# Third entry's first step two steps later, one piece a step; filter copy in 4 transfers

## The chip, the cores and the metric

The kernel runs on one core of one Trainium2 chip. The metric is the device time of a whole execution in microseconds (us). The kernel before has a median of 1882.88 us over 4 runs (1879.95, 1881.62, 1884.13 and 1885.79).

A core has engines with their own instruction queues: TensorE (PE, matmuls, with its weight loads PEld), VectorE (DVE), ScalarE (ACT), GpSimd (POOL) and SyncE (SP). Each works through its queue strictly in order; semaphores join the queues. SP, ACT and POOL also issue DMA transfers. Matmuls write to PSUM, from where ACT or DVE must copy results out before the buffer can be used again.

## The reference

Two computations follow each other. The first mixes along the sequence: a real Fourier transform, a product with a complex filter, and the inverse. The second is a feed-forward block with a SoLU activation and a layer norm.

```
X = rfft(x, axis=1)                       # x: 8 entries x 3136 x 256, f32
y = irfft(X * (filt_r + 1j * filt_i))     # filter: 1569 x 256, the same for all entries
h = y.reshape(25088, 256) @ w_in          # 25088 x 1024
solu = h * softmax(h)
ln = (solu - mean) / sqrt(var + 1e-6) * g_ln
out = ln @ w_out                          # 25088 x 256
```

## The kernel before

**The transform.** The length 3136 is split as 49 x 64 and the transform of an entry is done as matmuls in three stages with DRAM between them. *First* (L171): a load of x gives a piece of 98 rows x 4 columns x 256 channels; two matmul tiles (halves u = 0 and 1, PSUM tile `pa`) multiply it with a table, ACT copies each to SBUF (L180), and POOL stores the piece to the DRAM tile d1 (L183). An entry has 8 pieces. *Spectrum* (L189 to L241), 25 units of an entry's columns: a load of d1 (L193, SP), a forward matmul (`pb`), the product with the filter (ACT turns the parts at L214 and L215, DVE multiplies and adds at L222 to L224), an inverse matmul (`pc`), a copy by ACT (L236) and a store to the DRAM tile d2 (L241, POOL). A unit of two entries, or two units of one entry, go together. *Back* (L253): 8 pieces of d2 are loaded by SP, multiplied (`py`, two tiles a piece) and copied by ACT (L261) into the SBUF tile y, which holds two entries.

**The feed-forward part** goes over 196 blocks of 128 tokens, one a *step* k of the loop at L550. `hidden(k)` is 4 matmuls into h (L415), the maximum on DVE (L420) and the exponential on ACT (L423). `normalize(k)` is the product on DVE (L438) and the squares on ACT (L440). `turn` and `regroup` transpose over DVE and 4 small SP transfers (L448, L457), 4 to 5 steps later; `project(k - 6)` is 8 matmuls of the output (L475), so steps 0 to 5 have no projection. `prepare_w_out` scales the output weights on DVE in step 0, takes their mean on PE in step 1 (L383), and subtracts it on DVE in step 2.

**What comes when.** Entries 0 and 1 (group 0) run through first and spectrum before the loop, and entry 0 through back too, inside the block at L267, which also loads the weights as float64 words and converts them to float32 on DVE (`load_float64`, L280 to L300, ten instructions for a quarter of a weight matrix). The output weights are the four conversions j = 4 to 7; their loads (L275) are issued by POOL. In this block a scheduler of the framework orders the instructions of each engine; it sees the whole program, and it may take instructions from behind the block forward when nothing holds them. The loop stands under `tc.manual_schedule()`: there the order is as written.

In the loop the other entries' stages are spread over the steps. `GROUPS` (L37) gives for groups 1 to 4 the entries, (start, steps) of their first stage and (start, steps) of their spectrum; `spread(count, start, over)` puts piece i at step start + i * over // count. The jobs of a step come in this order: `first_of` (only steps 0 to 5: both halves of a piece and both halves of a back piece), hidden, turn, regroup, `early` (half 0), project, normalize, scale, then products, `late` (half 1), `stores` and `loads`. A load of rows is issued three steps ahead, or when the fourth load before it has been used: x pieces and back pieces share one pool of 4 buffers. PSUM has two tiles (`ps_t`) for `pa`, `py` and `pc` together, and SBUF two buffers for a first-stage result.

The filter is also needed in the loop, in an order of its own: L503 to L509 copy it from the inputs to the DRAM tile `f_dram`, in groups of 5 of the 25 planes, real and imaginary, upper and lower half, so 20 DRAM-to-DRAM transfers of 160 KB, four in each of steps 0 to 4, issued by POOL. `load_filter` (L399) reads it two steps before a unit's product.

Of the kernel before, what the change touches and what calls it, by code (L numbers as in the profile page):

```python
# [17 lines left out]
P = 128  # L18
B, S, C = 8, 3136, 256
# [5 lines left out]
NS, NQ = (N1 + 1) // 2, 64  # L25
NR = 2 * N1
NK = 4 * NS
NG = 5
# [7 lines left out]

GROUPS = [  # L37
    ((0, 1), None, None),
    ((2,), (0, 6), (9, 13)),
    ((3, 4), (6, 13), (22, 25)),  # L40
    ((5, 6), (32, 28), (64, 29)),
    ((7,), (94, 18), (116, 24)),
]
# [37 lines left out]
def kernel(  # L81
# [10 lines left out]
    nc = tc.nc  # L92
# [19 lines left out]
    f_dram = dram.tile([NS, NQ, 2, C], FP32, name="f_dram")  # L112
# [23 lines left out]
    def filter_rows(filt, quarter, s0, n):  # L136

        off, step = (s0 * C, C) if quarter % 2 == 0 else ((N1 - s0) * C, -C)
        return bass.AP(tensor=filt.tensor, offset=filt.offset + off,
                       ap=[[N1 * C, 32], [step, n], [1, C]])  # L140
# [104 lines left out]
    def fetch_back(e, ch, rows_pool):  # L245

        n, b = next((n, g[0].index(e)) for n, g in enumerate(GROUPS) if e in g[0])
        t4s[e, ch] = rows_pool.tile([P, NCH, C], FP32, name=f"t4_{e}_{ch}", tag="r")[0:NK]
        by_16(
            (nc.sync.dma_start, nc.sync.dma_start), t4s[e, ch],  # L250
            d2[n][b].rearrange("s (a n) c -> (s a) n c", a=4)[:, NCH * ch:NCH * ch + NCH, :])

    def back(e, ch, cb, evac):  # L253

        ps = ps_t.tile([P, 512], FP32, name=f"py_{e}_{ch}_{cb}", tag="t")
        psv = ps[:, 0:NCH * NR].rearrange("p (n r) -> p n r", r=NR)
        for i in range(NCH):
            nc.tensor.matmul(out=psv[:, i, :], lhsT=t4s[e, ch][:, i, cb * P:cb * P + P],  # L258
                             rhs=wi_t, start=True, stop=True)
        n0, t0 = NCH * ch, e % 2 * S  # L260
        evac(out=y[:, cb, t0:t0 + S].rearrange("p (r n) -> p n r", n=NH)[:, n0:n0 + NCH, :], in_=psv)  # L261
# [217 lines left out]
    def scale(k, ps):  # L479
# [14 lines left out]
    first_of, early, products, late, stores, loads = (  # L494
        [[] for _ in range(blocks + LAG)] for _ in range(6))

    def spread(count, start, over):
        return [start + i * over // count for i in range(count)]
# [1 line left out]
    def ahead(t, by):  # L500
        return loads[max(0, t - by)]

    for g in range(NS // NG):  # L503
        for k, filt in enumerate((filt_r, filt_i)):
            for half in range(2):
                loads[g].append(lambda filt=filt, half=half, k=k, g=g: nc.gpsimd.dma_start(
                    out=f_dram[NG * g:NG * g + NG, 32 * half:32 * half + 32, k, :].rearrange(
                        "s p c -> p s c"),
                    in_=filter_rows(filt, half, NG * g, NG)))  # L509

    row_loads = []

    for n in range(1, len(GROUPS)):
# [16 lines left out]
            stores[t + 1].append(lambda sp=sp, i=i: sp.store(i, nc.gpsimd.dma_start))  # L530
    for e in range(1, B):

        start, end = -(-S * (e - 1) // P) + (3 if e == 3 else 1), S * e // P - 1
        for ch, t in enumerate(spread(NH // NCH, start, end - start)):
            row_loads.append((t, lambda e=e, ch=ch: fetch_back(e, ch, pools["r"])))
            for cb in range(KD):
                (first_of if t < LAG else (early, late)[cb])[t].append(
                    lambda e=e, ch=ch, cb=cb: back(e, ch, cb, nc.scalar.copy))
# [62 lines left out]
```

## Time and profile before

| | us |
|---|---|
| median of 4 runs | 1882.88 |
| the profiled execution, its time | 1879.95 |
| its span, first to last instruction | 1878.0 |
| PE busy | 1801.0 (96%) |
| DVE busy | 1111.9 (59%) |
| ACT busy | 816.6 (43%) |
| POOL busy | 456.5 (24%) |
| start of the products of the first spectrum | 78.57 |
| start of the back matmuls of entry 0 | 147.93 |
| start of the first hidden matmul (step 0) | 181.25 |

The profiled execution is the lowest of the four runs. A step is recognised by its 8 records of L415 (a 128x512 f32 matmul makes two records of 429 ns start to start). In the table of windows, a row gives a stretch, its length, and the busy time of each engine with its number of records, then the clock that TensorE was granted (1.00 is full), the share of the DMA engines' time in use, and GB/s. A row of the timeline gives start, length, engine, line, operation, the tile written and those read, shapes, how many records are merged, and in brackets how long the engine had been idle and who released it. A row of waits gives the waiting engine and line, whom it waited for, the sum in us, how often, and the longest.

### The profile page before, as it was taken

What the parts mean: (1) busy time and instruction counts of PE and PEld (TensorE: products, weight loads), DVE (VectorE), ACT (ScalarE), POOL (GpSimd) and SP (SyncE); (2) the same over time, 40 slices, a digit from 0 to 9 for tenths busy, and PEclk for the clock granted to TensorE, in tenths of its full rate; (3) what the DMA queues carried; (4) which work ended last, traced back from release to release, by engine and by line L of the source; (5) the groups of instructions that cost most, each with busy time, mean ns of one, the idle gap of its engine ahead of it and who ended that gap; (6) DMA issues with size and microseconds to landing.
All of it is one profiled execution on the core that took longest, in us unless ns stands there. A gap on an engine that the chain in (4) does not pass through costs nothing.

```text
span 1878.0 us, 21235 instructions
## 1 busy us (share of the span) xinstructions
PE 1801.0 (96%) x6500; PEld 1166.4 (62%) x6500; DVE 1111.9 (59%) x1778; ACT 816.6 (43%) x1329; POOL 456.5 (24%) x1306
## 2 busy tenths in 40 slices
PE   6678899999999999999999999999999999999997
PEld 1126466666666666666666666666777676666665
DVE  0792445567666654566666655566665655666663
ACT  2363445544554534354554434444444343333331
POOL 3331333323323221132232121213222011110110
PEclk9796899999999999999999999999999999999999
DMA  9875489886778766566657656466684444434434
GB/s 276 276 228 159 141 227 253 235 196 165 197 198 206 186 148 149 133 160 167 165 147 177 147 132 156 100 162 158 159 181 112 112 93 111 114 83 101 103 89 101
DMA packets 314576, 300.77 MB, mean 160 GB/s; under 512 B 27602, under 2 KB 278995, under 8 KB 314465
## 3 DMA queue, kind: packets, MB, share of 16 engines
q1 hardware_dynamic: 283904, 206.69, 47.0%
q0 software_dynamic: 28768, 86.45, 15.5%
q10 hardware_dynamic: 1792, 6.29, 0.9%
q8 instruction: 53, 0.87, 0.2%
q14 instruction: 59, 0.48, 0.1%
HBM read 118.44 MB, written 81.40 MB: 106 GB/s over the span
## 4 chain that ended last, share of the span: by engine, by line
PE 90%; DMA 4%; issue 2%; POOL 1%; DVE 1%; ACT 1%; SPq 0%; POOLq 0%; DVEq 0%; ACTq 0%
PE po L475 36%; PE h L415 35%; PE py L258 7%; PE pa L177 5%; PE pb L203 4%; PE pc L233 3%; DMA x<-in_x_dram 2%; POOL d L241 1%; DMA d<-t 1%; DMA t<-d 1%; DVE nmax L420 0%; ACT e L423 0%; DVE solu L438 0%; ACT t L180 0%; POOL f L310 0%
## 5 line engine op out<-in xcount | busy, mean ns | idle before, releaser
L475 PE MATMUL po<-w_out_sb,solu_t 128*128 128x256 f32 x3136 | 713.4, 381 | 4.5 <-DVE ot L483 4.5
L415 PE MATMUL h<-w_in_sb,y 128*128 128x512 f32 x1568 | 707.7, 594 | 0.0
L475 PEld LDWEIGHTS po<-w_out_sb,solu_t 128*128 128x128 f32 x3136 | 593.7, 191 | 137.4 <-issue 57.4
L420 DVE TENSOR_REDUCE nmax<-h 128x1 f32<-128x1024 f32 x196 | 239.8, 1223 | 450.7 <-PE h L415 450.7
L415 PEld LDWEIGHTS h<-w_in_sb,y 128*128 128x128 f32 x1568 | 294.5, 191 | 314.6 <-issue 304.2
L423 ACT ACTIVATE e<-h,nmax 128x1024 f32<-128x1024 f32 x196 | 218.4, 1114 | 603.3 <-DVE nmax L420 603.3
L440 ACT ACTIVATE e<-solu,nmu 128x1024 f32<-128x1024 f32 x196 | 225.1, 1148 | 293.9 <-DVE solu L438 287.8
L438 DVE SCALAR_TENSOR_TENSOR solu<-e,rsum,h 128x1024 f32<-128x1024 f32 x196 | 251.0, 1281 | 7.1 <-DVE rsum L435 0.2
L448 DVE STREAM_TRANSPOSE turn<-solu 128x1024 f32<-128x1024 f32 x196 | 241.9, 1234 | 0.0
L241 POOL DMA_DIRECT2D d<-g x101 | 76.0, 753 | 565.8 <-ACT g L236 555.4
L258 PEld LDWEIGHTS py<-wi_t,t 100*128 100x128 f32 x1024 | 146.7, 213 | 59.6 <-issue 41.7
L177 PE MATMUL pa<-x,wf_t 98*100 98x512 f32 x256 | 140.8, 657 | 27.1 <-DMA x<-in_x_dram 20.5
L258 PE MATMUL py<-wi_t,t 100*128 100x98 f32 x1024 | 146.3, 295 | 16.5 <-DMA t<-d 9.2
L467 POOL COPY rs_t<-rs 32x1 f32<-32x1 f32 x784 | 141.7, 181 | 35.7
L483 DVE TENSOR_SCALAR ot<-po,rs_t 128x256 f32<-128x256 f32 x196 | 94.5, 482 | 84.0 <-PE po L475 73.0
L222 DVE TENSOR_TENSOR p<-pb,f 128x512 f32<-128x512 f32 (+1 forms) x101 | 69.2, 686 | 122.3 <-ACT i L215 121.1
L203 PE MATMUL pb<-t,de 128*128 128x512 f32 (+1 forms) x250 | 107.2, 527 | 13.7 <-DMA t<-d 13.0
L261 ACT COPY y<-py 128x392 f32<-128x392 f32 x128 | 106.8, 835 | 30.4 <-PE py L258 30.3
L461 POOL TENSOR_SCALAR rs<-var 128x4 f32<-128x4 f32 x49 | 9.6, 197 | 451.7 <-ACT e L440 449.9
L233 PE MATMUL pc<-p,de 128*128 128x512 f32 (+1 forms) x250 | 103.8, 513 | 9.7 <-DVE p L224 8.2
L177 PEld LDWEIGHTS pa<-x,wf_t 98*100 98x100 f32 x256 | 44.9, 183 | 89.9 <-issue 59.5
L180 ACT COPY t<-pa 100x512 f32<-100x512 f32 (+1 forms) x112 | 71.1, 640 | 65.6 <-PE pa L177 59.3
(51 smaller groups left out, 853.1 us busy)
## 6 DMA issues: line engine op xcount, KB each, us to landing
solu_t<-turn SPq DMA_DIRECT2D x784, 128.0 KB
t<-d SPq DMA_DIRECT2D x99, 256.0 KB
d<-g POOLq DMA_DIRECT2D x99, 256.0 KB, 4.1
out_dram<-ot SPq DMA_DIRECT2D x196, 128.0 KB
x<-in_x_dram SPq DMA_DIRECT2D x64, 384.0 KB
t<-d SPq DMA_DIRECT2D x64, 384.0 KB
d<-t POOLq DMA_DIRECT2D x48, 384.0 KB, 5.1
f<-f_dram POOLq DMA_DIRECT2D x104, 128.0 KB, 4.3
```

The lines of the kernel that those rows point to most:

```text
L177: nc.tensor.matmul(out=ps[0:NK, j], lhsT=wf_t, rhs=self.xs[i][0:NR, 2 * u:2 * u + 2, :], start=True, stop=True)
L203: nc.tensor.matmul(out=ps[:, w * j:w * j + w, :], lhsT=de[:, s + j, 0, :], rhs=t2[:, w * j:w * j + w, :], start=True, stop=True)
L233: nc.tensor.matmul(out=ps[:, w * j:w * j + w, :], lhsT=de[:, s + j, 1, :], rhs=pt[:, w * j:w * j + w, :], start=True, stop=True)
L258: nc.tensor.matmul(out=psv[:, i, :], lhsT=t4s[e, ch][:, i, cb * P:cb * P + P], rhs=wi_t, start=True, stop=True)
L415: nc.tensor.matmul(out=h[:, half, :], lhsT=y[:, c, P * t:P * t + P], rhs=w_in_sb[:, c, 512 * half:512 * half + 512], start=(c == 0), stop= ...
L420: nc.vector.tensor_reduce(out=nmax, in_=h, axis=AX.X, op=ALU.max, negate=True)
L423: nc.scalar.activation(out=e, in_=h, func=AFT.Exp, bias=nmax, accum_out=esum)
L438: nc.vector.scalar_tensor_tensor(out=solu, in0=e, scalar=rsum, in1=hs.pop(k), op0=ALU.mult, op1=ALU.mult, accum_out=nmu)
L440: nc.scalar.activation(out=e, in_=solu, func=AFT.Square, bias=nmu, scale=-float(DFF), accum_out=variances[g][:, i:i + 1])
L448: nc.vector.transpose(out=turns[g][:, :, i, :], in_=solus.pop(k).rearrange("p (f j) -> p f j", j=32))
L467: nc.gpsimd.tensor_copy(out=rss[g][32 * i:32 * i + 32, c:c + 1], in_=rs[32 * c:32 * c + 32, i:i + 1])
L475: nc.tensor.matmul(out=ps, lhsT=solu_t[:, f, :], rhs=w_out_sb[:, f, :], start=(f == 0), stop=(f == KF - 1))
```

## The change

Three things are altered in the loop's plan:

- Entry 2 (group 1): its first stage moves from (0, 6) to (2, 7). The pieces stood at steps 0, 0, 1, 2, 3, 3, 4, 5; they now stand at 2, 2, 3, 4, 5, 6, 7, 8. Its spectrum moves from steps 9 to 21 to steps 11 to 23.
- Entries 3 and 4 (group 2): first from (6, 13) to (9, 13), spectrum from steps 22 to 46 to steps 24 to 48. The back pieces of entry 2 begin at step 27 instead of 26, those of entry 3 at 53 instead of 52.
- `f_dram` is written by 4 transfers of 800 KB, one in each of steps 0 to 3, instead of 20 of 160 KB.

```
 GROUPS = [
     ((0, 1), None, None),
-    ((2,), (0, 6), (9, 13)),
-    ((3, 4), (6, 13), (22, 25)),
+    ((2,), (2, 7), (11, 13)),
+    ((3, 4), (9, 13), (24, 25)),
     ((5, 6), (32, 28), (64, 29)),
...
-    for g in range(NS // NG):
-        for k, filt in enumerate((filt_r, filt_i)):
-            for half in range(2):
-                loads[g].append(lambda filt=filt, half=half, k=k, g=g: nc.gpsimd.dma_start(
-                    out=f_dram[NG * g:NG * g + NG, 32 * half:32 * half + 32, k, :].rearrange(
-                        "s p c -> p s c"),
-                    in_=filter_rows(filt, half, NG * g, NG)))
-
+    def copy_filter(k, half):
+        nc.gpsimd.dma_start(
+            out=f_dram[:, 32 * half:32 * half + 32, k, :].rearrange("s p c -> p s c"),
+            in_=filter_rows((filt_r, filt_i)[k], half, 0, NS))
+
+    for k in range(2):
+        for half in range(2):
+            loads[2 * k + half].append(lambda k=k, half=half: copy_filter(k, half))
...
-        start, end = -(-S * (e - 1) // P) + (3 if e == 3 else 1), S * e // P - 1
+        start, end = -(-S * (e - 1) // P) + {2: 2, 3: 4}.get(e, 1), S * e // P - 1
```

The built program shows one more difference, ahead of the loop. The scheduler's order for the first spectrum is another one: on POOL, the two copies of the filter's real part are taken forward, one before the first store of L241 and one between the 15th and the 16th; on POOL, the loads of the last two quarters of the output weights come earlier (behind the 12th and the 18th store instead of behind the 15th and the last); on DVE, 17 more of the conversion instructions stand before the last product of the first spectrum (33 instead of 16, with 9 behind it instead of 26); on ACT, copies of L236 stand in bunches of three where they alternated with L214 and L215. In step 0 the first x piece is no longer loaded ahead of the back pieces of entry 0.

## The prediction

> **What bounds the kernel now.** I read the page's first two parts, then the windows cut at the starts of the steps, then PE's timeline where a window is not full, and last the waits of DVE, PE and ACT in the first spectrum. From the page:
>
> ```profile
> span 1878.0 us, 21235 instructions
> PE   6678899999999999999999999999999999999997
> ```
>
> and from the windows (all engines; then PE alone, for steps 0, 1, 2, 4, 6 and 7):
>
> ```profile
> 78.57:137.49 58.92, 48.62 (x95) 15.80 (x94) 56.83 (x94) 42.06 (x72) 23.70 (x34) 0.98 0.74 229
> 252.43:1838.70 1586.27, 1585.76 (x5914) 1053.48 (x5913) 976.47 (x1542) 706.77 (x1161) 376.63 (x1153) 1.00 0.63 153
> ...
> 181.25:194.66 13.41, 8.85 (x29) 0.85 0.67 211
> 194.66:204.65 9.99, 9.99 (x29) 0.86 0.36 107
> 204.65:219.68 15.03, 10.62 (x34) 0.89 0.56 159
> 224.86:231.23 6.37, 5.40 (x14) 1.00 0.08 33
> 234.66:252.43 17.77, 15.55 (x49) 0.81 0.87 212
> 252.43:261.07 8.64, 8.64 (x30) 1.00 0.98 299
> ```
>
> From step 7 to the last hidden matmul PE is busy 1585.76 of 1586.27 us at full clock. Step 7 lasts 8.64 us and holds 8 records of 429 ns (hidden), 16 of 216 (projection) and 4 of 429 (pa), 8.60 in all: matmuls back to back. The change alters no matmul, so in this stretch it can only add waits. What it can win or lose lies before 252.43: in the first spectrum, where DVE is busy 56.83 of 58.92 us and so sets the pace, and in steps 0 to 6, where PE is not full. The timeline there:
>
> ```profile
> 136.81 0.67 DVE L224 TENSOR_TENSOR p<-p,i 128x512 f32<-128x512 f32 x1
> 137.41 0.68 DVE L292 SCALAR_TENSOR_TENSOR power<-raw,power 128x512 int32<-128x512 int32 x1
> 151.25 0.69 DVE L300 TENSOR_TENSOR w_out_sb<-w_out_sb,power 128x512 f32<-128x512 f32 x1
> ...
> 147.93 27.60 PE L258 MATMUL py<-wi_t,t 100*128 100x98 f32 x128 [9.20 <-DMA t<-d]
> 175.32 6.09 PE L177 MATMUL pa<-x,wf_t 98*100 98x512 f32 x8
> 191.13 3.74 PE L258 MATMUL py<-wi_t,t 100*128 100x98 f32 x16 [4.56 <-ACT t L180]
> 194.66 4.99 PE L415 MATMUL h<-w_in_sb,y 128*128 128x512 f32 x8
> 214.38 3.66 PE L177 MATMUL pa<-x,wf_t 98*100 98x512 f32 x4 [4.41 <-ACT t L180]
> 242.19 2.03 PE L258 MATMUL py<-wi_t,t 100*128 100x98 f32 x8 [2.21 <-ACT t L180]
> 244.01 5.91 PE L475 MATMUL po<-w_out_sb,solu_t 128*128 128x256 f32 x16
> ```
>
> The last product of the first spectrum is at 136.81; DVE then still converts weights until 151.94, which nobody waits for, while the last product goes through pc, a copy, a store (issued at 139.64, landed 2.7 us later) and the load to py at 147.93. In the steps the brackets show one pattern: two tiles fill `ps_t`, ACT frees them only behind that step's exponential and squares, and PE stands 4.56, 4.41, 0.97 (step 4) or 2.21 us. After the long ones PE runs at half clock: py x16 takes 3.74 instead of 1.99, h 4.99 instead of 3.60, pa 3.66 instead of 1.88, py x8 2.03 instead of 1, po 5.91 instead of 3.62. Waits in the first spectrum (78 to 140 us):
>
> ```profile
> DVE p L222 <- ACT i L215: 6.8, 9, 5.0
> PE pc L233 <- DVE p L224: 7.2, 15, 1.2
> ACT g L236 <- DMA d<-g: 1.0, 1, 1.0
> ```
>
> DVE's own idle time inside the stretch is 1.8 us (6.8 less the 5.0 before its first product): it has no room for more work.
>
> **A. The first spectrum.** As built, the changed program puts 17 more conversion instructions before the last product: 6 of the second conversion (692, 421, 418, 687, 686 and 685 ns by the groups of 139 to 152 us), all 10 of the third (5.30 us) and one of the fourth (421 ns), 9.3 us by their lengths. DVE starts the next 0.60 us after a long one and 0.34 after a short one where they are mixed with others: 8 x 0.60 + 9 x 0.34 = 7.9. I take 8.0; at most 9.3, at least 6.1 if all of the 1.8 us is filled. The cover is gone by the same move: behind 137 us these instructions ran beside the store and the load. Everything to the first hidden matmul (back of entry 0, 27.60 us of PE) moves by as much.
>
> Three smaller terms. (1) ACT now does three copies of L236 in a row with three buffers, so the next waits for a store's landing, which took 2.5 to 6.4 us (median 3.9) in this stretch; DVE waits behind. Also an 800 KB copy now runs beside the loads and stores, at a DMA share of 0.74 that was 0.94 to 1.00 from 90 to 100 us. One such wait cost 1.0 before; I take +1.8, between 0 and 4. (2) Where 7 to 9 conversions stand between products, PE gets gaps of 2.5 to 3 us instead of at most 1.4. Gaps of 2.21 and more cost the clock in the steps; a pc at half clock takes 2.06 instead of 1.10. I take two spells, +2.2; 0 to 5. (3) The last weight load no longer stands before the last loads, whose landing decided 147.93: -1.0; 0 to -1.5. Sum A: 8.0 + 1.8 + 2.2 - 1.0 = +11.0, ends 4.6 and 18.3.
>
> [...]
>
> **B. Steps 0 to 9.** Lost before: idle 4.56 + 4.41 + 0.97 + 2.21 = 12.2, half clock 1.75 + 1.39 + 1.78 + 1.03 + 2.29 = 8.2, together 20.4. The 8 pa records before step 0 (6.09 us for 3.43 of work) paid the end of the half clock; the first hidden matmuls take their place and pay it alike.
>
> Lost after, from the same durations, counted from the end of the first hidden (its end to the weights' scaling is nmax 1.23, exp 1.30, rsum 0.6, product 1.38, scaling 2.1, some 6.5):
> - Step 1: py 1.8 and hidden 3.43 end at 5.2; the mean over the weights waits to 6.5: 1.3 idle.
> - Step 2 has two pieces, four tiles: the third waits for ACT behind squares 1 and the weights' mean: 1.7.
> - Step 3 has pa, pa, py, py: the pattern of step 0 before, 4.6 idle and 3.1 at half clock.
> - Step 5: as step 4 before, 1.0.
> - Step 9 has two pa and a py, as step 6 before: 2.2, without the half clock, since a projection follows on either side.
>
> Sum 13.9. So B = 13.9 - 20.4 = -6.5. At best (no half clock, step 9 at 0.9) 9.3 is lost, B = -11.1; at worst a second and longer half-clock spell, 19.8, B = -0.6. Moving three pieces from the loose steps to steps 6 to 8 costs their 5.2 us there and frees it here, already in this count.
>
> **C. The filter copy itself.** 20 issues of 0.58 to 0.65 us were 11.8 us of POOL, beside waits of POOL on ACT of up to 38.5 us; 4 issues cost between 2.4 and 12 us. PE never waited for them: 0. Their first reader moves from step 7 to 9. [...] In this trace they land in 3.6 to 6.3 us, several at a time, and nobody waits.
>
> **D. The later stages.** The first load of a spectrum now stands in the step of its last piece's store (steps 8 and 21), as does the first back load of entry 2 (step 24, the store of the last unit). On SP it waits for copy, two POOL issues and landing, 0.6 + 1.1 + 4 to 7 us into the next step; behind it are that step's 4 regroup transfers (2.6 to 5.6 us of issue), whose projection comes two steps later, after 8.6 + 8.6 + 3.5 us. 21 against 9 to 14 and their landing: I take 0, at worst 5.
>
> **Sum.** 11.0 - 6.5 + 0 + 0 = +4.5. Against the profiled execution (1879.95, its span and 1.95 around it) 1884.4. That execution is 2.9 below the median; the half-clock spells that make up 8 us of its loss need not fall alike in every run, so I carry the difference to the median: 1882.88 + 4.5 = 1887.4. Within 0.2% is 3.8 us either way, about what a measurement here can tell from no change.
>
> **Rivals.** *The two cancel.* The order on DVE costs its 8 less 1, the clock holds in the spectrum and ACT's bunches cost nothing: A = 7, B = -6.5 to -8: 1882 to 1883. For it: PE kept full clock from 82 to 144 us before, through gaps of up to 1.4 us. Against it: the gaps double.
> *The steps win (other side).* One mechanism: PE's stands behind ACT vanish and with them the half clock, B = -11, while A is no more than its bare 7: -4, 1879; it decides from A below B's size less 3.8. For it: 8.2 us of half clock hang on three stands, of which one remains. Against it: one pattern of 4.6 is kept.
> *SP stands.* If a landing takes 7 us and regroup's issue 5.6 at steps 21 to 25, a projection comes late, up to three times: +5 to +10 on top, 1892 to 1897. For it: issues of 5.2 to 5.6 us at 270 to 330 us. Against it: 21 us of room.
> *The change does not do what it says:* the copies in 4 leave POOL free, but it was free; that is C, zero in every case.
>
> **Numbers.** Forecast (slower by 2 to 9 us) 0.44, SP 0.06, cancel 0.28, steps win 0.22. Slower 0.50, same 0.28, faster 0.22. The range leaves a tenth on either side: from 1878, between the steps-win case and the ends of B, to 1895, A's upper part with B at -3.
>
> **What would show it.** A: the first py of entry 0 starts at about 159 instead of 147.93, the last L224 at about 147, and DVE's conversions end near 152 as before. B: the first hidden matmul follows py at once; step 0 to 6 have one stand over 4 us (step 3, <-ACT t L180), short ones of 1 to 2; step 6 near 9 us. D: no PE wait for solu_t after step 9, step lengths equal to their matmuls. I am wrong if py starts before 153 (DVE had room), if half clock shows in 80 to 140 us for more than 10 us (A larger), or if windows after step 9 are not full.

## The result, and the profile after

The changed kernel has a median of 1889.86 us over 47 runs (1883.24 to 1897.80), the kernel before 1884.58 over 74 runs beside them (1879.21 to 1890.71). The ratio is 1.0026 with a 95% interval of 1.0020 to 1.0032: slower by 4.9 us (3.8 to 6.0), where +4.5 was forecast, 1887.4 against 1882.88. The profiled execution has a span of 1888.7 us, 10.7 more than that of before; what part of the 10.7 belongs to the change is the first thing to settle.

The first spectrum, as windows (length, busy time of PE, PEld, DVE, ACT, POOL with records, then granted clock, DMA share, GB/s). The first row runs from the first `pb` to the end of the last product, the second from there to the first `py` of entry 0; then steps 0 to 3 by their places in the profile (a place begins at the step's first hidden matmul and ends at the next one's, so the next step's `first_of` is its tail), then steps 9 and 13, and the rest:

```profile
span 1888.7 us, 21209 instructions
...
79.75:155.22 75.47, 57.24 (x98) 19.48 (x98) 65.28 (x111) 42.94 (x74) 25.91 (x37) 0.87 0.65 209
155.22:165.43 10.21, 1.10 (x3) 0.33 (x3) 4.63 (x10) 0.58 (x1) 0.72 (x1) 0.63 0.72 211
192.82:199.34 6.52, 6.52 (x25) 3.73 (x25) 1.23 (x1) 1.11 (x2) 0.00 (x0) 0.80 0.01 3
199.34:212.36 13.02, 10.59 (x34) 5.84 (x33) 7.62 (x19) 7.82 (x14) 1.06 (x2) 1.00 0.23 62
212.36:225.62 13.26, 8.85 (x30) 5.53 (x28) 6.67 (x14) 4.82 (x8) 3.69 (x7) 0.76 0.70 215
225.62:232.76 7.14, 7.14 (x14) 2.97 (x14) 1.52 (x2) 1.03 (x2) 0.00 (x0) 0.72 0.55 173
270.19:283.99 13.80, 12.43 (x49) 7.49 (x48) 4.47 (x7) 6.26 (x12) 1.86 (x4) 1.00 0.64 152
314.29:327.70 13.41, 12.32 (x43) 7.37 (x42) 6.28 (x11) 6.48 (x11) 3.08 (x6) 1.00 1.05 269
327.70:1849.00 1521.30, 1520.79 (x5672) 1010.51 (x5671) 939.67 (x1484) 676.32 (x1111) 358.02 (x1099) 1.00 0.62 151
```

The same first window of before:

```profile
75.28:137.48 62.20, 51.91 (x98) 16.76 (x98) 56.82 (x94) 43.23 (x74) 23.69 (x34) 0.95 0.74 230
```

DVE has 111 records instead of 94, the 17 conversion instructions, and is busy 8.46 us longer; the stretch is 13.27 longer, so DVE is idle 4.81 us more (10.19 instead of 5.38). PE's clock is 0.87 instead of 0.95, and its 98 matmuls take 57.24 instead of 51.91. The waits of DVE and of PE in it (sum, times, longest):

```profile
DVE p L222 <- ACT i L215: 10.5, 6, 8.7
DVE p L222 <- PE pc L233: 4.8, 7, 1.0
...
PE pc L233 <- ACT g L236: 10.9, 5, 2.9
```

The middle row is new, 4.8 us, as much as the added idle time: DVE stands because `pc`, which reads the buffers of the products, is not through. `pc` in turn waits for ACT's copies out of PSUM, 10.9 us where it was 1.4 before. PE's timeline shows where, and what it costs behind (start, length, line, tiles, records merged, idle before):

```profile
102.77 3.32 PE L233 MATMUL pc<-p,de 128*128 128x512 f32 x4 [2.66 <-ACT g L236]
...
115.20 1.98 PE L233 MATMUL pc<-p,de 128*128 128x512 f32 x4 [2.90 <-ACT g L236]
...
127.64 3.42 PE L233 MATMUL pc<-p,de 128*128 128x512 f32 x4 [2.31 <-ACT g L236]
...
145.32 3.78 PE L233 MATMUL pc<-p,de 128*128 128x512 f32 x4 [2.76 <-ACT g L236]
...
165.43 27.60 PE L258 MATMUL py<-wi_t,t 100*128 100x98 f32 x128 [8.96 <-DMA t<-d]
192.82 4.92 PE L415 MATMUL h<-w_in_sb,y 128*128 128x512 f32 x8
...
210.57 1.96 PE L177 MATMUL pa<-x,wf_t 98*100 98x512 f32 x4 [2.43 <-ACT t L180]
...
222.09 3.73 PE L258 MATMUL py<-wi_t,t 100*128 100x98 f32 x16 [4.41 <-ACT t L180]
...
326.76 1.10 PE L177 MATMUL pa<-x,wf_t 98*100 98x512 f32 x2 [1.09 <-ACT g L236]
```

Four records of `pc` take about 1.9 us at full clock (1.90 at 90.56). Behind three of these four stands (a stand is a time in which PE waits) they take 3.32, 3.42 and 3.78 at a granted clock of 0.57, 0.57 and 0.50; behind the longest one, at 115.20, they take 1.98 at 1.00. DVE's waits for `pc` go with the clock and not with the length of the stand:

```profile
104.42 0.69 DVE L222 TENSOR_TENSOR p<-pb,f 128x512 f32<-128x512 f32 x1 [0.43 <-PE pc L233]
...
129.75 0.69 DVE L222 TENSOR_TENSOR p<-pb,f 128x512 f32<-128x512 f32 x1 [0.61 <-PE pc L233]
131.10 0.69 DVE L222 TENSOR_TENSOR p<-pb,f 128x512 f32<-128x512 f32 x1 [0.66 <-PE pc L233]
...
147.43 0.69 DVE L222 TENSOR_TENSOR p<-pb,f 128x512 f32<-128x512 f32 x1 [0.52 <-PE pc L233]
149.13 0.69 DVE L222 TENSOR_TENSOR p<-pb,f 128x512 f32<-128x512 f32 x1 [1.01 <-PE pc L233]
```

These five, 3.2 us, stand behind the three slow ones. The other two (1.04 at 88.38 and 0.47 at 91.69) are at the start of the stretch, where a `pc` of two records at 86.20 still took 2.08 us at a clock of 0.50. Behind the `pc` at 115.20 DVE has no wait for it.

From 192.82 on, PE's rows show the steps: hidden directly behind `py`, one stand of 2.43 at the two pieces of step 2, one of 4.41 with half clock (0.50) behind it in step 3, and one of 1.09 in step 13.

By stage, after against before:

| stage | before | after | difference |
|---|---|---|---|
| up to the first `pb` | 75.28 | 79.75 | +4.5 |
| first `pb` to first `py` of entry 0 | 72.65 | 85.68 | +13.0 |
| first `py` to the start of step 10 | 132.99 | 118.56 | -14.4, of which -6.0 is work moved behind step 10 (12 pa and 4 pb records: 12 x 0.429 + 0.86) |
| step 10 to the end | 1597.10 | 1604.68 | +7.6, of which +6.0 is that work |

So the first spectrum gives +13.0, steps 0 to 9 give -8.4, and something behind step 10 gives +1.6: +6.2. The remaining +4.5 lies in front of the first `pb`, where the instruction order of both programs is the same; the second profile of the changed kernel, below, has it at -1.7. The +6.2 is a difference of two single profiles, and the medians differ by less (4.9 by the ratio): the profiled execution of before is one of its faster ones.

### The profile page after: what moved, and what is told of

The parts are those of the page before. It is cut to its first block, busy times and chain, and to the rows that moved or that the text cites. A ratio compares the mean times of both kernels' runs of the same rounds, so it can differ in the third digit from the quotient of the medians.

```text
span 1888.7 us, 21209 instructions
## 1 busy us (share of the span) xinstructions
PE 1806.3 (96%) x6500; PEld 1167.8 (62%) x6500; DVE 1111.6 (59%) x1778; ACT 815.5 (43%) x1329; POOL 446.8 (24%) x1290
## 4 chain that ended last, share of the span: by engine, by line
PE 89%; DMA 4%; issue 2%; DVE 2%; POOL 1%; ACT 1%; SPq 0%; DVEq 0%; ACTq 0%; POOLq 0%
PE po L475 35%; PE h L415 35%; PE py L258 7%; PE pa L177 5%; PE pc L233 4%; PE pb L203 4%; DMA d<-t 2%; DMA x<-in_x_dram 1%; POOL d L241 1%; DMA t<-d 1%; DVE nmax L420 1%; DMA d<-g 0%; DVE solu L438 0%; ACT e L423 0%; ACT t L180 0%
## 5 line engine op out<-in xcount | busy, mean ns | idle before, releaser
L475 PEld LDWEIGHTS po<-w_out_sb,solu_t 128*128 128x128 f32 x3136 | 592.0, 190 | 136.8 <-issue 57.5
L241 POOL DMA_DIRECT2D d<-g x101 | 75.4, 747 | 576.8 <-ACT g L236 564.4
L233 PE MATMUL pc<-p,de 128*128 128x512 f32 (+1 forms) x250 | 108.4, 537 | 15.1 <-ACT g L236 10.9
```

The lines of the kernel that those rows point to most:

```text
L233: nc.tensor.matmul(out=ps[:, w * j:w * j + w, :], lhsT=de[:, s + j, 1, :], rhs=pt[:, w * j:w * j + w, :], start=True, stop=True)
L475: nc.tensor.matmul(out=ps, lhsT=solu_t[:, f, :], rhs=w_out_sb[:, f, :], start=(f == 0), stop=(f == KF - 1))
```

## Experiments

All ratios are against the kernel before, run beside them. "Between" is the number of conversion instructions that DVE has between the first and the last product (before 16, changed 33). Two explanations of the first spectrum's loss are set against each other: the *order theory* (where the conversions stand on DVE costs it) and the *traffic theory* (the copies' bytes beside the spectrum's loads and stores cost it). The first four runs undo or separate the parts of the change, the rest vary the order or the number of copies, and two take a second profile of a program. Times from "first `pb` to last product" end at the start of the last product; the windows end with it.

**The copy alone.** The old `GROUPS` and starts, with `copy_filter` in steps 0 to 3. The scheduler leaves the first spectrum as it was.

```
-    ((2,), (2, 7), (11, 13)),
-    ((3, 4), (9, 13), (24, 25)),
+    ((2,), (0, 6), (9, 13)),
+    ((3, 4), (6, 13), (22, 25)),
...
-{2: 2, 3: 4}.get(e, 1)
+(3 if e == 3 else 1)
```

> Only the filter's DRAM copy is changed (4 transfers of 800 KB in steps 0 to 3); entry 2's pieces stay where they were, and the order of the first spectrum is that of before (26 conversion instructions behind the last product, no copy taken forward). The order theory and the traffic theory both put the loss into the first spectrum and the gain into the steps, so both expect no change: 0, within 2 us, and the first py of entry 0 some 72 to 73 us after the first pb. The rival that four long copies cost time by themselves in the loop (POOL's queue, DMA bandwidth in steps 0 to 9) expects the whole difference of the change here, +4.9 us.

Measured: 1.0007 (0.9997 to 1.0018), no difference that can be told. First `pb` to first `py` took 73.3 us, and the stands of before are all there (4.57, 4.41, 0.97 and 2.22).

**The moved stages alone.** The new `GROUPS` and starts, with the 20 transfers of before.

> Only the stages are moved; the copy stays in 20 transfers of 160 KB. The scheduler takes 8 of them (1.28 MB, against 1.6 MB in the changed kernel) forward into the first spectrum, but puts only one more conversion instruction before the last product instead of 17. Order theory (DVE's place for the conversions costs the +13.0 us of the first spectrum): 13.0 / 17 = +0.8 there, -8.4 in the steps, so -7.6 us against before, about 1877; first py 73 to 74 us after the first pb. Traffic theory (the copies beside the spectrum's loads and stores cost it): 13.0 x 1.28 / 1.6 = +10.4, in all +2.0, about 1886.5; first py about 83 us after the first pb.

Measured: 0.9963 (0.9949 to 0.9976), -7.0 us. The window from the first `pb` to the end of the last product:

```profile
75.97:138.19 62.22, 52.25 (x98) 16.76 (x98) 57.49 (x95) 43.05 (x74) 28.61 (x42) 0.95 0.78 245
```

One record more on DVE, eight more on POOL (the 1.28 MB of copies that were taken forward), the DMA share up from 0.74 to 0.78, and the length is that of before. The copies' bytes cost nothing that can be seen here; the traffic theory falls for this place. With the first run this makes the table of two by two: copy alone +0.07%, stages alone -0.37%, both +0.26%. The loss belongs to neither part. It comes out of the order that the scheduler finds when both are there.

**The copies two steps later.** The changed kernel with one line altered:

```
-            loads[2 * k + half].append(...)
+            loads[2 + 2 * k + half].append(...)
```

> As the changed kernel, but the four copies stand in steps 2 to 5 instead of 0 to 3. None is taken forward, and the conversions stand as before (26 behind the last product). Both theories say that the loss of the first spectrum is gone and the gain of steps 0 to 9 stays: -8.4 us against before, about 1876 (ratio 0.9955), first py 72 to 73 us after the first pb, first hidden matmul directly behind py, lost time in steps 0 to 9 about 15 us against 23.6. The rival that the moved steps themselves cost the first spectrum its time (the x loads that no longer stand ahead of the back pieces) expects no gain: +4.9, about 1889.

Measured: 0.9962 (0.9949 to 0.9974), median 1875.97, -7.2 us. Against the changed kernel this one line is worth 0.64%, 12.1 us.

```profile
74.63:136.86 62.23, 51.53 (x98) 16.91 (x98) 56.85 (x94) 43.27 (x74) 23.70 (x34) 0.95 0.71 223
136.86:147.60 10.74, 1.10 (x3) 0.33 (x3) 7.27 (x17) 0.59 (x1) 2.12 (x3) 0.73 0.80 237
...
193.61 3.73 PE L177 MATMUL pa<-x,wf_t 98*100 98x512 f32 x4 [2.43 <-ACT t L180]
197.14 4.95 PE L415 MATMUL h<-w_in_sb,y 128*128 128x512 f32 x8
...
208.22 3.73 PE L258 MATMUL py<-wi_t,t 100*128 100x98 f32 x16 [4.42 <-ACT t L180]
```

The first spectrum is that of before within 0.03 us. The steps are those of the changed kernel with the same stands, but here the stand of 2.43 is followed by half clock (3.73 and 4.95 instead of 1.96 and 3.60), so step 10 begins 121.4 us behind the first `py` instead of 118.6. This kernel is faster than before and than the changed one.

**All four copies in step 0.**

```
-            loads[2 * k + half].append(...)
+            loads[0].append(...)
```

> As the changed kernel, but all four copies of 800 KB stand in step 0. The scheduler takes all four forward into the first spectrum (3.2 MB instead of 1.6), with the same 17 conversion instructions before the last product. Order theory: the same as the changed kernel, +4.9 us against before, first py 85 to 86 us after the first pb. Traffic theory: twice the loss there, 26 - 8.4 = +17.6 us, about 1902, first py about 98 us after the first pb.

Measured: 1.0095 (1.0076 to 1.0115), +17.9 us, as the traffic theory had it in sum. But the time is not where that theory puts it. First `pb` to last product took 75.9 us (74.8 in the changed kernel); the missing 10 us lie behind the last product, where the first `py` comes 20.8 us later instead of 10.9. The chain of waits there, of this kernel and then of the changed kernel (start, length, what), and the SP queue's own rows:

```profile
157.80 6.57 DMA d<-g
164.37 0.02 issue
164.38 10.83 DMA t<-d
...
159.44 3.74 SPq L145 DMA_DIRECT2D t<-d  x7
164.38 0.25 SPq L146 DMA_DIRECT2D t<-d  x1
```

```profile
157.38 4.95 DMA d<-g
162.33 0.02 issue
162.35 2.94 DMA t<-d
...
157.31 1.34 SPq L145 DMA_DIRECT2D t<-d  x3
162.35 0.92 SPq L146 DMA_DIRECT2D t<-d  x3
```

A back piece is loaded in two transfers, 96 rows (L145) and the last 4 (L146); only the 4 wait for the last store. In this kernel the scheduler put seven large loads ahead of the first small one, in the changed kernel three. The small one then landed 10.83 us after its issue instead of 2.94. Of the 10 us this is 7.9, and the last store's landing (6.57 instead of 4.95) is 1.6.

Four more transfers of 384 KB than in the changed kernel were issued ahead of the small one, 1.57 MB. From 164.3 to 172.1 us the DMA engines moved 239 to 284 GB/s; at some 250 GB/s the 1.57 MB take, as an estimate, 6.3 of the 7.9 us. Whether the small transfer stood in line behind them or shared the bandwidth with them, no run shows.

**Three copies in step 0, the fourth in step 3.**

```
-            loads[2 * k + half].append(...)
+            loads[(0, 0, 0, 3)[2 * k + half]].append(...)
```

> As the changed kernel, with three copies in step 0 and the fourth in step 3. The order of all engines in the first spectrum is that of the run with all four in step 0, but no copy stands between the last two stores: three are taken forward (2.4 MB), ahead of stores 0, 15 and 21. If the 10 us by which that run was slower than the changed kernel come from the one copy ahead of the last store (its rows are in front of the first back load), they go: first py 10 to 11.5 us behind the last product, first pb to last product 75 to 76, against before +4.9 to +6, about 1890. If they come from the bytes, three of four copies leave half of what lies between the changed kernel and that run: +11, about 1896.

Measured: 1.0032 (1.0019 to 1.0045), +6.0 us, with first `pb` to last product 74.9 and `py` 10.8 behind it. In this kernel no copy stands ahead of the last store, and SP has two large loads ahead of the first small one. Three copies in the first spectrum cost what two cost, as far as these runs can tell. The expectation blamed the copy ahead of the last store; the traces point to the loads' order on SP, which changed along with it. These runs did not separate the two, but the store behind that copy landed only 1.6 us later.

**One copy forward, half the conversions.** The copies in steps 0, 2, 3 and 4: 25 between.

```
-            loads[2 * k + half].append(...)
+            loads[(0, 2, 3, 4)[2 * k + half]].append(...)
```

> As the changed kernel, with the copies in steps 0, 2, 3 and 4: one copy is taken forward, and 25 conversion instructions stand between the first and the last product (9 more than before, where the changed kernel has 17 more). Order theory: DVE's own time 9 x 0.50 = 4.5, and DVE's waits for pc between none and 9 / 17 of 4.8 = 2.5: first pb to last product 66.0 to 68.5 us; against before -7.2 + 4.5 to 7.0, so -2.7 to -0.2, about 1880 to 1882. Rival (copies): -1.2, the same within the error; this run is for the size of an instruction.

Measured: 1.0004 (0.9989 to 1.0018). The window is 69.58 us with DVE busy 61.23, so 7.4 longer than before: 4.4 busy and 3.0 idle, a little over the upper end that was given.

**Two g buffers.**

```
-("p", 2), ("g", 3)
+("p", 2), ("g", 2)
```

> As the changed kernel, with two buffers instead of three for the results of the first spectrum (the tiles g that ACT writes in L236). ACT can't make three copies in a row any more; the scheduler puts all 42 conversion instructions between the first and the last product (9 more than the changed kernel, 26 more than before) and takes the same two copies forward. Order theory: 26 x 0.50 = 13.0 us of DVE on top of 61.5: 74.5 if the bunches of three were what made DVE wait for pc (4.8 us in the changed kernel), up to 82 if those waits go with the number of conversions (26 / 17 of 4.8 more). Against before -7.2 + 13.0 to 20.3: +6 to +13, about 1888 to 1896. Rival (copies): as the changed kernel, +4.9, first pb to last product 74 to 75 us, so only a value above 77 speaks against it here.

Measured: 1.0065 (1.0046 to 1.0085), +12.2 us, with the window at 81.80, DVE busy 70.92. The order theory's upper end holds. The expectation's other branch is wrong in its ground: the scheduler made the bunches longer, one of four copies and one of five, and ACT now waits inside them for the stores' landing.

```profile
74.57:156.37 81.80, 58.51 (x98) 19.39 (x98) 70.92 (x119) 42.50 (x74) 26.08 (x36) 0.83 0.64 205
...
PE pc L233 <- ACT g L236: 10.4, 6, 2.9
...
ACT g L236 <- DMA d<-g: 6.8, 6, 2.5
```

**Three p buffers.** The same line with `("p", 3), ("g", 3)`: 30 between.

> As the changed kernel, with three buffers instead of two for the products p and i of the first spectrum. 30 conversion instructions stand between the first and the last product (14 more than before, 3 fewer than in the changed kernel), two copies are taken forward. In the changed kernel DVE waited 4.8 us for pc, which holds a buffer of p. If the two buffers carry these waits: 61.5 + 14 x 0.50 = 68.5 us from first pb to last product, against before -7.2 + 7.0 = 0, about 1884. If the waits are only moved on (pc late behind ACT's copies in bunches, DVE idle as long in another row): 68.5 + 3 to 4.8 = 71.5 to 73.3, +3 to +4.6, about 1888.

Measured: 1.0012 (0.9999 to 1.0025), +2.3 us, first `pb` to last product 73.2. DVE's wait for `pc` fell only to 2.9 us and its wait for ACT rose; PE still waited 9.2 us for ACT's copies. So the products' two buffers are not what causes the idle time (10.0 us against 10.2); most of it moves to another row.

**One copy written into the first spectrum; fewer conversions between.** The kernel with the late copies, but the first copy stands in the code of the block ahead of the last store. The scheduler took it to the front and left 8 between.

```
+            if i == NS - 1:
+                copy_filter(0, 0)
             sp.store(i, nc.gpsimd.dma_start)
...
+            if (k, half) != (0, 0):
                 loads[2 + 2 * k + half].append(...)
```

> As the run with the copies in steps 2 to 5, but the first of the four copies (800 KB) is written into the code of the first spectrum. The scheduler puts it ahead of the first store, as in the changed kernel, and leaves only 8 conversion instructions between the first and the last product (16 before, 33 in the changed kernel), with 34 behind it. Order theory, at 8.5 / 17 = 0.50 us of DVE for an instruction: first pb to last product 61.5 - 4.0 = 57.5 us, and -7.2 - 4.0 = -11.2 us against before, about 1871. Rival (a copy taken forward costs time of itself, half of the 12.1 us for one of two): -7.2 + 6.0 = -1.2, about 1881, first pb to last product 67 to 68 us.

Measured: 0.9995 (0.9983 to 1.0007). The gain of 11 us was not there, and first `pb` to last product took 62.6 us, not 57.5. DVE is busy 54.85 of the window's 63.30 us, two less than before, and idle 8.45, three more.

**The same once more.**

> The run with the first copy ahead of the first store once more, for a second profile: its profiled execution took 1878.38 us, the fastest of its twelve (median 1883.9). If what hides between is the start of the first spectrum (DMA ahead of it) then the first pb is later than 78.1 here and first pb to last product stays at 62.6; if it is the clock in the spectrum, first pb to last product is 65 or more.

This execution took 1888.64 us: first `pb` at 84.03, and 65.0 from there to the last product. Both things that the expectation held apart had happened.

The second is the clearest row on the clock in this case, since both executions are of one program. Up to 26.3 us behind the first `pb` their products start at the same times within 0.02 us. Then PE stands 2.69 and 2.68 us for ACT's copies. In the first execution the `pc` behind it takes 1.98 us, in this one 3.49, and by 35 us DVE is 1.3 us late. Behind the next stand, again of 2.69 and 2.68, it takes 3.53 and 3.78, and what follows in this one is slow too (`pb` of two records 1.92 instead of 1.02); DVE ends 2.4 us late. The clock is 0.89 instead of 0.94 and DVE's busy time the same (54.88 and 54.85). So half clock on PE lengthens this stretch by itself, here by 1.3 us at the first place and 1.1 at the second.

As to the start: the copy was issued at 68.5 and 72.3 us in the two profiles, ahead of the first spectrum's own loads, and no other kernel here has one there. Whether it is what made the start late, or whether the two executions are at the late end of the scatter below, is left open.

**Conversions held back.** The kernel with the late copies, but the loads of the first two quarters of the output weights wait for units 19 and 21:

```
+                nc.gpsimd.tensor_copy(out=raw.bitcast(FP32)[0:1, 0:1, 0], in_=behind[0:1, 0, 0:1])
...
+            if i in (19, 21):
+                held[4 if i == 19 else 5] = sp.gs[i]
+                begin(4 if i == 19 else 5)
             sp.store(i, nc.gpsimd.dma_start)
-        for j in (4, 5):
-            begin(j)
```

> As the run with the copies in steps 2 to 5, but the loads of the first two quarters of the output weights are held back: a one-element copy on POOL writes into the load's buffer from the results of units 19 and 21, so the load can't start before them. Only 4 conversion instructions remain between the first and the last product, 38 behind it, beside the store, the load and the 27.6 us of back matmuls. Order theory: first pb to last product 61.5 - 12 x 0.50 = 55.5 us unless PE (51.5 us busy there) paces it from 57 on; against before -7.2 - 4.5 to -6.0, so -11.7 to -13.2, about 1870. Rival (the order on DVE is not what costs): -7.2, about 1875. Point at which it turns: 38 instructions and two loads one after the other end near 160 us; if they ended behind 170, the weights' scaling in step 0 and the mean in step 1 would wait.

Measured: 0.9970 (0.9958 to 0.9982), -5.7 us: no better than the late copies alone (-7.2), where 4.5 to 6 more were expected.

```profile
72.61:134.06 61.45, 51.15 (x98) 17.30 (x98) 52.70 (x82) 42.61 (x73) 24.09 (x35) 0.94 0.75 232
...
PE pc L233 <- DVE p L224: 5.5, 6, 2.0
PE pc L233 <- ACT g L236: 2.9, 2, 2.1
```

Twelve records fewer and 4.1 us less of DVE shortened the stretch by 0.8 us. Above 16 conversions more work on DVE lengthens this stretch; below 16 less work hardly shortens it. What then sets its 61 to 63 us is not shown; one of DVE's own waits in this run, 1.5 us, is for the load of the weights.

**The changed kernel again.**

> The changed kernel once more, for a second profile. The instruction order up to the first pb is the same in all these kernels but the two with the conversions held or the first copy written in early, while that pb started between 74.6 and 79.8 us. If that is scatter of the execution, this profile has it anywhere from 74 to 80; if the change makes it late, near 79.8 again. First pb to last product 74.8 in both cases.

```profile
73.58 2.05 PE L203 MATMUL pb<-t,de 128*128 128x512 f32 x2 [13.46 <-DMA t<-d]
159.09 27.60 PE L258 MATMUL py<-wi_t,t 100*128 100x98 f32 x128 [9.08 <-DMA t<-d]
...
73.58:148.77 75.19, 58.53 (x98) 19.63 (x98) 65.45 (x111) 42.94 (x74) 25.91 (x37) 0.85 0.71 221
```

The same program began its first spectrum 6.2 us earlier than in the first profile; the rest is the same within 0.5 us (its execution took 1885.34 us). The eleven profiles whose order up to there is the same have that start anywhere from 73.58 to 79.75. The +4.5 in front of the first `pb` is scatter.

**The size of an instruction.** The windows from the first `pb` to the end of the last product, by the number between:

| kernel | between | ACT's copies in bunches | length | DVE busy | DVE idle |
|---|---|---|---|---|---|
| conversions held | 4 | 11 | 61.45 | 52.70 | 8.8 |
| copy written in early | 8 | 11 | 63.30 | 54.85 | 8.5 |
| the same, second profile | 8 | 11 | 65.69 | 54.88 | 10.8 |
| before | 16 | 7 | 62.20 | 56.82 | 5.4 |
| late copies | 16 | 7 | 62.23 | 56.85 | 5.4 |
| stages alone | 17 | 9 | 62.22 | 57.49 | 4.7 |
| copies in 0, 2, 3, 4 | 25 | 14 | 69.58 | 61.23 | 8.4 |
| three p buffers | 30 | 17 | 73.86 | 63.90 | 10.0 |
| changed | 33 | 17 | 75.47 | 65.28 | 10.2 |
| changed, second profile | 33 | 17 | 75.19 | 65.45 | 9.7 |
| three in step 0 | 33 | 17 | 75.59 | 65.30 | 10.3 |
| all four in step 0 | 33 | 17 | 76.55 | 65.50 | 11.1 |
| two g buffers | 42 | 16 | 81.80 | 70.92 | 10.9 |

From 16 conversions up, DVE's busy time goes up by 0.5 to 0.6 us for each; from 4 to 16 by 0.34. The idle time goes roughly with the order on ACT: the third column counts, of the 25 copies of L236 in the built order, those that stand next to another one with no L214 or L215 between. It is about 5 us with 7 to 9 of them, 8.4 to 10.8 with 11 to 14, and 9.7 to 11.1 with 16 or 17. No run altered ACT's order by itself, so this part is a correlation over eleven kernels with a wait that fits it, not more. The two profiles with 8 between show that the order does not fix it: the idle time differs by 2.4 us with the same order, by the clock.

## Why the prediction was right, point by point

The sign and the size were right, and the sum came nearer than its terms. Against the two profiles, the two large terms were each too small by about 2 us, which cancelled, and a term put at 0 was 1.6 (B's miss is within what profiles of the same steps scatter); that +4.5 lies so near the measured +4.9 is in part luck.

**A, the first spectrum: +11.0 forecast, +13.0 in the first profile and +12.9 in the second.** The late copies alone take it away, from 16 conversions on the stretch grows with their number, and three copies of 800 KB cost about as much as two: the order is what costs, as forecast. The first `py` was forecast at about 159 us; it came at 165.43 and, in the second profile, at 159.09, but there with a start that is 1.7 us earlier than before's. Its terms:

- 17 conversion instructions, 8.0 forecast: 8.46 of DVE's busy time.
- Term (1), ACT's bunches of three, 1.8 by waits for a store's landing: no such wait occurred in the changed kernel. This mechanism was wrong. What the bunches do is that `pc` finds both tiles of PSUM taken until ACT comes to its copies (10.9 us of PE).
- Term (2), two spells of half clock, 2.2: this is where the added idle time is. There were three spells, by the `pc` rows of 3.3 to 3.8 us, and 3.2 of DVE's 4.8 us of waiting for `pc` stand behind them, 1.1 a spell as forecast. (The rest, 1.5 at the start of the stretch, is in neither term; in the second profile it does not come, and 3.9 us stand behind slow `pc` rows.) That half clock costs this much with nothing else altered is what the two profiles of one program above show. The gaps before them, 2.31 to 2.76 us, are of the forecast size, but in them PE waits for ACT's copies and not for DVE's conversions; the gap of 2.90 us kept its clock and cost DVE nothing. The clock from 80 to 140 us was 0.89 instead of 0.99, an estimated 13 us at half clock; more than 10 was a sign that the prediction named for a larger A. Together 4.0 was forecast for the two terms and 4.8 of added idle time measured; that (1) was wrong and (2) too small by one spell nearly cancelled, by luck.
- Term (3), -1.0 for the last weight load that no longer stands before the last loads: -0.2 (10.90 us from the start of the last product to `py`, 11.12 before).

**B, steps 0 to 9: -6.5 forecast, -8.4 measured (-7.8 in the second profile).** The stands were placed well: step 2 1.7 forecast and 2.43 measured, step 3 4.6 and 4.41 with half clock behind, step 5 1.0 and 0.97, none of 2.2 in step 9 but 1.4, at full clock as forecast (1.70 lost in all). The wait of the weights' mean in step 1 (1.3 forecast) did not come. In sum 15.2 us were lost where 13.9 was forecast. The step that missed is the other side of the subtraction. The working left out the 2.5 us that the pa ahead of step 0 lost to the half clock behind `py` (6.09 us at a clock of 0.59), since the hidden matmuls would pay them alike; they paid 1.3 (4.92 us for 3.60). Small losses in the old steps that are not stands made up the rest: 23.6 instead of 20.4. (The best case of B is mis-added: its terms give a loss of 9.5 us, not 9.3.) All this is of single profiles, and the clock makes them scatter: from the first `py` to step 10 the moved steps took 118.6 to 121.8 us in their twelve profiles, and the first hidden matmuls paid 0.8 to 2.4 us in them; the old steps took 133.0 and 135.6 in their two. The forecast for B is not shown to be wrong by more than that.

**C, the copy itself: 0 forecast.** The copy alone measured 1.0007, within no change. Its effect is only through the order, which the prediction had in A.

**D, the later stages: 0 forecast, +1.6 measured, a miss.** No wait for SP came, and the windows are full from step 14 to the end. That a window after step 9 would not be full was one of its signs of being wrong, and step 13 is such a window. It takes 13.41 us for the same 43 records that took 12.14 in step 10 before; here is that row:

```profile
280.92:293.06 12.14, 12.14 (x43) 7.37 (x42) 7.30 (x12) 6.61 (x11) 2.97 (x5) 1.00 1.01 237
```

The timeline after has 1.09 us at its end, <-ACT g L236: two pieces and a `pc` share two tiles of PSUM, and the second piece's tile waits for the copy of `pc`. The prediction looked for late transfers on SP and did not count PSUM tiles in that step. The second profile of the changed kernel has the same wait, 1.2 us.

**The rivals.** That the steps win was not right for this kernel, but its condition, an A smaller than B's size less 3.8, is what the late copies make, with A near nothing: -7.2 us. That the two cancel needed A at 7; it was 13. No wait of PE behind SP's transfers came in the steps.

Equal stands of PE did not cost equal clock. In the first spectrum the stand of 2.90 us left the four records of `pc` behind it at 1.98 us in the first profile of the changed kernel, and at 3.78 in its second. In step 2, the stand of 2.43 us cost no clock in the first profile (`pa` 1.96, clock 1.00), and 1.77 + 1.35 us in the kernel with the late copies. What decides it, no run here shows. Nor did a long busy stretch alone bring full clock back: `py` took 27.60 us (27.59 in two) in every one of the fourteen profiles, with 128 matmuls back to back, at a granted clock of 0.50 in the profile of before and in the first of the changed kernel.

## What to carry to other kernels

A scheduler that takes work from behind a block forward ties edits together: where a transfer is placed in a later loop decided the order of vector instructions a hundred microseconds earlier, so compare the built order, not the diff, and try moving the trigger by a step or two before giving the whole change up. The busy time of the engine that sets the pace tells what more work costs (0.5 us an instruction here), but not what less work gains; for that, ask which wait ends next when its own is gone. When a matmul comes late, look at the clock behind the wait as well as at the wait: here a stand cost the rest of the kernel something where half clock followed it. Count PSUM tiles by step whenever stages are moved against each other, not only the transfers.

## What the runs showed that was not expected

- Taking 12 conversion instructions (4.1 us of DVE) out of a stretch where DVE was 91% busy shortened it by 0.8 us only. DVE's idle time rose by 3.4 us at the same time; which wait makes up all of that is not shown.
- 1.28 MB of copies in eight transfers ran beside the first spectrum's loads and stores without lengthening it (62.22 us against 62.20), and a third 800 KB added 0.1 us (75.59 against 75.47), while the small load behind seven large ones instead of three landed 7.9 us later at the point where everything waited for it.
- One program, run twice, took 2.4 us longer from the first `pb` to the last product (65.0 instead of 62.6) with the same instruction order and the same busy time of DVE, because the `pc` behind two equal stands of PE ran at half clock more often.
- The start of the first spectrum scattered over 6 us between executions of programs with the same order up to it; a comparison of two single profiles must be made by stage, from an event on.
